# A long convolution and an attention on one core: four streams in the planner, sums by accumulating transfers, skip term in the first tap

## The chip, the core and the metric

The kernel runs on one core of a Trainium2 chip. A core has TensorE (PE; its weight loads are shown as PEld), VectorE (DVE), ScalarE (ACT), GpSimd (POOL) and SyncE (SP), each with its own instruction order, and 16 DMA engines that serve the queues of SP, ACT and POOL. Engines wait for each other through semaphores only. The metric is the device time of one execution in microseconds.

## What is computed

Two independent heads, joined in the last axis. The first is a long convolution: a kernel K of 2048 taps for each of 576 channels is made from a sum of 128 complex exponentials, and the input u is convolved with it, causally, with a skip term.

```
P = exp(logdA[:, :, None] * l)                       # D=576, N=128, L=2048
K = einsum("dn,dnl,dn->dl", Cc, P, dB).real
y = irfft(rfft(pad(u)) * rfft(pad(K)))[:L] + u * Dskip
```

The second is an attention over S=2048 with 32 query heads of 18 and one key and value head, fp32.

```
scores = einsum("bhqd,bkd->bhqk", q, k) * Dh**-0.5
o = einsum("bhqk,bkd->bhqd", softmax(scores), v);  out = o @ wo
```

## The kernel before

The attention runs over 4 chunks of 512 queries, 8 groups of 4 heads, 16 key blocks of 128 keys and 2 head pairs: 1024 score tiles (`pairs`). A score tile is two fp16 matmuls of 512 columns (L532) into one of 3 PSUM buffers; ScalarE makes exponentials of 1024 columns from it (L543); two half products of 256 columns (L845) add values times exponentials into `ops`. Beside this run the query projections (`qproj`), whose results go through DRAM by POOL's queue and come back as `aug` by SP's, and the output projections (`outproj`).

The convolution goes over 12 blocks of 48 channels (`Conv`). `front` (L1238) makes a block's kernel: `factors` (exponentials and sines on ScalarE once for two blocks, the second block parked in DRAM), `tables` (products on VectorE) and `kgen` (L1220; matmuls at L1231 into PSUM, copied to `ksb` by VectorE), then a trip through DRAM into `kt`. `back` (L1294) takes the forward transforms of the input and of the kernel (`transform`, L1263: TensorE matmuls lh, VectorE combinations `sc`), multiplies them in four taps (products `acc` and `pt`, sums of `pt` into `acc`, all on VectorE), combines three products into a complex one (`acc`, then `sv` and `w`), and takes the inverse transform (`iy`) to which the skip product `u` is added. Three accumulating transfers a block (L1303, L1316, L1338) and one plain (L1302) go by POOL's queue. All of it and the projections share one PSUM bank (`bank`, L235).

The order of the instructions on PE, ACT, DVE and POOL is fixed when the program is built, by a planner in the kernel itself. `Clock` keeps the planned time of TensorE (`t`), VectorE (`v`) and ScalarE (`a`). The works are generators (`Stream`): each yields before a step whether it is a TensorE step ("p"), a VectorE step ("v") or a wait ("w", "b"), and the time from which it is ready. `main` (L778) takes three score tiles a round, and between rounds `fill` (L801) puts in steps of the side work and the convolution as a credit allows. `turn` (L1396) runs the convolution as two streams, `back(k)` and `front(k+1)`, and starts the next pair when both have ended. Where VectorE copies out of the bank, the planned VectorE time is set to TensorE's (`evacuate`, L1255) and the copy is entered at once.

```
def evacuate(self):
    K = self.k
    K.v = max(K.v, K.t)
```

After the last product, what is left of the convolution is put in (`drain`, L1431), then `finish` (L642) normalizes the last heads and adds the last sums of the output.

Of the kernel before, what the change touches and what calls it, by code (L numbers as in the profile page):

```python
# [25 lines left out]
KT = [(k * 128, 128) for k in range(5)]  # L26
DT = KT[:4] + [(512, 64)]
# [11 lines left out]
LIMIT = 60.0  # L39

# [5 lines left out]
RATE = 6.983  # L46
PACE = 1.7672
AHEAD = 0.4952
TOTAL = 604.4861
LAST = 813.2825  # L50
DEFER = 0.378
NAUG = 5
LEFT = 1.1655
CAP = 1.5491
DEBT = 0.6604
GROUP = 0.1377
HOLD = 0.3071
LEAD = 1.8204
MOST = 0.4269
LEAST = 0.3048  # L60
NEAR = 1.3779
SLOPE = 0.851
SOON = 1.3672
URGENT = 8.8421
BACK = 2
HELD = 0
GAP = 0.2663
GAP_NEW = 0.3191
# [13 lines left out]

class Clock:
# [6 lines left out]
    def __init__(self):  # L90
        self.t = self.v = self.a = 0.0
        self.work = 0.0
        self.s = [0.0] * NS
        self.fill = 0.0
        self.due = self.last = 1e9

    def near(self):

        return NEAR if self.t + SOON > min(self.due, self.last) else 0.0

    def pe(self, cost, *after):
        self.t = max(self.t, *after) + cost if after else self.t + cost

    def act(self, cost, after=0.0):
        self.a = max(self.a, after) + cost
        return self.a

    def filled(self):

        self.fill = self.v + 0.25  # L110
        self.due = 1e9

    def dve(self, n, rate, after):
        cost = 0.068 + rate * n + (0.119 if after else 0.0)
        self.v += cost
        self.work += cost


class Vector:
# [5 lines left out]
    def cost(self, rate, out, *ins, n=None):  # L125

        place = lambda x: (x.name, x.offset)
        self.k.dve(math.prod((n or out).shape[1:]), rate, self.last in [place(x) for x in ins if hasattr(x, "offset")])
        self.last = place(out)
# [9 lines left out]
    def tensor_scalar(self, out, src, *a, **k):  # L139
        self.cost(0.527e-3, out, src, *a)  # L140
# [18 lines left out]
class Stream:  # L159
# [26 lines left out]
    def go(self, step, credit, lock=None):  # L186

        k = self.k
        ready = self.ready if self.kind != "p" or self.holds else max(self.ready, k.fill)
        if not self.live or self.kind == "b" or self.kind == "p" and (credit <= 0 or k.t < ready or lock not in (None, self)):  # L190
# [19 lines left out]
class Attention:  # L210
# [7 lines left out]
    def __init__(self, tc, ctx, aps, clock):  # L218
        self.tc, self.nc, self.a, self.k = tc, tc.nc, aps, clock
# [15 lines left out]
    def bank(self, n, name):  # L235
        self.k.pe(0.0, self.k.fill)
# [10 lines left out]
    def setup(self, tp, conv):  # L247
# [4 lines left out]
        self.sel = conv.con[:, 2 * NF:]  # L252
# [122 lines left out]
    def second(self):  # L375
# [3 lines left out]
        K.pe(0.86)  # L379
        self.last()  # L380
        K.pe(0.86)
        K.v = max(K.v, K.t)
# [6 lines left out]
    def maxima(self):  # L389
# [4 lines left out]
        K.pe(1.1)  # L394
        K.v = max(K.v, K.t)
# [4 lines left out]
    def values(self):  # L400
# [4 lines left out]
        K.pe(1.0)  # L405
        K.v = max(K.v, K.t)
# [8 lines left out]
    def qproj(self, c, m, xt):  # L415
# [5 lines left out]
        for f in range(n // 256):  # L421
            sl = slice(f * 256, f * 256 + 256)
            yield "p", K.fill, False
            ps = self.bank(256, f"q{c}_{m}_{f}")
            for k in range(5):
# [6 lines left out]
                K.pe(0.465)  # L432
                self.q_left -= 1
                self.units += 1
                K.due = K.t + 0.465 * (4 - k)
                if k < 4:
                    yield "p", 0.0, True
            K.v = max(K.v, K.t)
# [21 lines left out]
    def queries(self, c, m, qh, ql, aw):  # L460
# [18 lines left out]
        yield "p", max(K.v + 0.4, K.fill), False  # L479
# [10 lines left out]
        K.pe(0.15)  # L490
        K.v = max(K.v, K.t + 0.3)
# [33 lines left out]
    def scores(self, i, c, pr, kb, cost):  # L525
# [7 lines left out]
        K.pe(cost, K.s[i % NS])  # L533
        return ps, K.t + 0.27

    def exponentials(self, i, c, pr, kb, ps, ready, free):
        nc, K = self.nc, self.k
        K.s[i % NS] = K.act(0.925, max(ready, free)) + 0.1
# [7 lines left out]
    def gather(self, c, g, o_ps):  # L546
        nc = self.nc
        o_sb = self.p2.tile([P, CT], F32, tag="o", name=f"o{c}_{g}", bufs=1)
        self.k.v = max(self.k.v, self.k.t)
        self.V.tensor_copy(o_sb, o_ps)  # L550
        self.o_free = self.k.v + 0.3
        nc.sync.dma_start(self.od[c][g * P:(g + 1) * P, :], o_sb)

    def normalize(self, c, ms):
# [11 lines left out]
        yield "v", K.t + 6.0, False  # L566
# [6 lines left out]
        yield "v", K.v + 3.0, False  # L573
# [8 lines left out]
        for m in ms:  # L582
            mn = MT[m][1]
            yield "v", K.t + 5.0, False
            V.tensor_tensor(o[:mn, m, :], o[:mn, m, :], tiles[m][:mn, :], op=ALU.mult)
            self.scaled[m] = K.v + 0.3
# [3 lines left out]
    def outproj(self, c):  # L590
        nc, V, K = self.nc, self.V, self.k
        o = self.oT
        self.o_left += 40
        yield "p", max(self.scaled[4], K.fill), False
# [183 lines left out]
    def main(self, conv, flag):  # L778
# [81 lines left out]
        for r in range(0, len(pairs), NS):  # L860
# [45 lines left out]
            if r:  # L906
                fill(free())
# [643 lines left out]
```

## Time and profile before

| | us |
|---|---|
| median of three runs | 1216.06 (1213.11 to 1217.59) |
| the profiled execution | 1217.0 |
| its span, first to last instruction | 1215.2 |
| PE busy in the span | 1099.6 |
| ACT busy | 1035.3 |
| DVE busy | 961.1 |
| POOL busy | 95.5 |

The profile is of one execution. Busy time of an engine is the time in which one of its instructions ran; issuing transfers doesn't count as busy except on POOL. PEclk is the share of its full speed (2.4 GHz) that TensorE's clock was granted. In a row, `out<-in` names tiles by the names of the program, `Lnn` is a line of the kernel; the line can be that of a helper (L133 is every addition or product of two tiles on VectorE, L207 every matmul in four column strips).

### The profile page before, as it was taken

What the parts mean: (1) busy time and instruction counts of PE and PEld (TensorE: products, weight loads), DVE (VectorE), ACT (ScalarE), POOL (GpSimd) and SP (SyncE); (2) the same over time, 40 slices, a digit from 0 to 9 for tenths busy, and PEclk for the clock granted to TensorE, in tenths of its full rate; (3) what the DMA queues carried; (4) which work ended last, traced back from release to release, by engine and by line L of the source; (5) the groups of instructions that cost most, each with busy time, mean ns of one, the idle gap of its engine ahead of it and who ended that gap; (6) DMA issues with size and microseconds to landing.
All of it is one profiled execution on the core that took longest, in us unless ns stands there. A gap on an engine that the chain in (4) does not pass through costs nothing. (4 is left out here: it accounts for less than half of the span.)

```text
span 1215.2 us, 41325 instructions
## 1 busy us (share of the span) xinstructions
PE 1099.6 (90%) x17974; PEld 534.7 (44%) x17974; DVE 961.1 (79%) x1722; ACT 1035.3 (85%) x1092; POOL 95.5 (8%) x151
## 2 busy tenths in 40 slices
PE   7999999899999899999989999986789998999924
PEld 2454454345445344545444545432344543454412
DVE  7868979977975885995989596873779589869875
ACT  5899899899889978999999999999689999999700
POOL 1010201110110100110010000020000000000000
PEclk9999999999999999999999999998899999999967
DMA  8432343343323324322341312232042124241122
GB/s 295 130 121 69 105 118 90 113 134 110 91 58 97 97 74 154 103 66 89 95 165 49 120 51 82 75 80 110 21 149 58 69 67 151 72 130 42 46 66 68
DMA packets 54253, 117.87 MB, mean 97 GB/s; under 512 B 7628, under 2 KB 24925, under 8 KB 52787
## 3 DMA queue, kind: packets, MB, share of 16 engines
q1 hardware_dynamic: 43571, 88.62, 21.6%
q0 software_dynamic: 10064, 26.19, 9.3%
q8 instruction: 143, 2.34, 0.8%
q10 hardware_dynamic: 432, 0.37, 0.1%
q14 instruction: 43, 0.35, 0.1%
HBM read 54.58 MB, written 41.46 MB: 79 GB/s over the span
## 5 line engine op out<-in xcount | busy, mean ns | idle before, releaser
L543 ACT ACTIVATE P<-s 128x1024 f32<-128x1024 f32 x992 | 938.9, 1036 | 95.5 <-PE s L532 90.0
L845 PE MATMUL ops<-P,v_sb 128*32 128x256 f32 x8192 | 536.6, 383 | 4.1 <-DVE o L137 3.6
L845 PEld LDWEIGHTS ops<-P,v_sb 128*32 128x32 f32 x8192 | 247.2, 110 | 187.3 <-issue 53.2
L532 PE MATMUL s<-aug,kaug 55*128 55x512 f16 x2048 | 303.2, 382 | 28.8 <-ACT P L543 25.6
L532 PEld LDWEIGHTS <-kaug 55*128 55x128 f16 x2048 | 95.2, 94 | 248.4 <-issue 202.1
L207 PE MATMUL op<-wo_sb,oT 126*32 126x288 f32 (+1 forms) x1128 | 84.7, 417 | 8.3 <-DVE ob L137 5.9
L207 PE MATMUL q<-x,wq_sb 128*32 128x256 f32 x1200 | 80.1, 395 | 7.4 <-DVE un L145 4.2
L137 DVE COPY ksb<-kg 128x192 f32<-128x192 f32 x48 | 17.4, 363 | 70.9 <-PE kg L1231 70.9
L207 PE MATMUL iy<-w,dft_sb 128*32 128x192 f32 x768 | 40.8, 344 | 24.6 <-DVE w L133 23.8
L133 DVE TENSOR_TENSOR tab<-tab,tt 128x576 f32<-128x576 f32 (+1 forms) x72 | 59.1, 821 | 1.5
L133 DVE TENSOR_TENSOR tab<-sum,r 128x576 f32<-128x576 f32 (+1 forms) x72 | 58.8, 817 | 0.0
L133 DVE TENSOR_TENSOR tt<-f,sum 128x576 f32<-128x576 f32 (+1 forms) x72 | 58.8, 817 | 0.0
L133 DVE TENSOR_TENSOR tab<-r,dif 128x576 f32<-128x576 f32 (+1 forms) x72 | 58.8, 816 | 0.0
L133 DVE TENSOR_TENSOR tab<-tab 128x576 f32<-128x576 f32 (+1 forms) x72 | 58.7, 815 | 0.0
L133 DVE TENSOR_TENSOR acc<-acc,pt 128x864 f32<-128x864 f32 (+2 forms) x72 | 54.4, 755 | 1.7
L133 DVE TENSOR_TENSOR pt<-us,ks 128x864 f32<-128x864 f32 (+2 forms) x72 | 54.2, 753 | 0.8
L207 PEld LDWEIGHTS q<-x,wq_sb 128*32 128x32 f32 x1200 | 36.8, 113 | 40.6 <-issue 13.2
L207 PEld LDWEIGHTS op<-wo_sb,oT 126*32 126x32 f32 (+1 forms) x1128 | 32.4, 111 | 47.3 <-issue 10.7
L1231 PE MATMUL kg<-tab 128*32 128x64 f32 x2304 | 42.9, 224 | 9.0 <-DVE tab L133 7.2
L1302 POOL DMA_DIRECT2D us<-us x12 | 6.7, 559 | 510.4 <-issue 227.0
L1231 PEld LDWEIGHTS kg<-tab 128*32 128x32 f32 x2304 | 37.8, 113 | 20.4 <-DVE tab L133 7.8
L676 ACT ACTIVATE o_last<-ops 128x256 f32<-128x256 f32 x2 | 0.8, 384 | 53.5 <-issue 51.9
(169 smaller groups left out, 1055.0 us busy)
## 6 DMA issues: line engine op xcount, KB each, us to landing
park<-two SPq DMA_DIRECT2D x6, 1944.0 KB
us<-us POOLq DMA_DIRECT2D x24, 384.0 KB, 3.9
od<-o SPq DMA_DIRECT2D x31, 256.0 KB
aug<-qd SPq DMA_DIRECT2D x124, 54.0 KB
u<-u SPq DMA_DIRECT2D x12, 480.0 KB
kd<-ksb SPq DMA_DIRECT2D x12, 384.0 KB
kt<-kd SPq DMA_DIRECT2D x48, 96.0 KB
ks<-ks POOLq DMA_DIRECT2D x12, 384.0 KB, 4.8
```

The source lines that it names most:

```text
L133: return self.v.tensor_tensor(out, a, b, **k)
L137: return self.v.tensor_copy(out, src)
L207: nc.tensor.matmul(ps[j:e], w[:, j:e], x, start=start, stop=stop, tile_position=(0, j))
L532: nc.tensor.matmul(ps[:, j, :], self.kaug[r, kb * P:(kb + 1) * P], t[r, :], start=True, stop=True)
L543: nc.scalar.activation(pt, ps, AF.Exp, scale=SCALE / UNIT ** 2)
L676: nc.scalar.activation(o_sb[:, half[f]], o_ps[:, half[f]], AF.Copy)
L845: nc.tensor.matmul(o_ps[32 * j:32 * j + 32, cs], self.v[:, kb, :], pts[2 * n + j // 2][:, j % 2, cs], start=(kb + f == 0), stop=(kb + f == ...
L1231: nc.tensor.matmul(ps[32 * g:32 * g + 32, d, :], t[:, :32], t[:, 32:], start=(j == 0), stop=(j == 1), tile_position=(0, 32 * g))
L1302: nc.gpsimd.dma_start(us[:, 0:4, :], us[:, 4:8, :])
```

## The change

The planner's `Clock` gets a time for every engine and for transfers: it keeps for each part of each tile when it was written and read last, with a cost for a transfer by bytes and rows. A stream's readiness is asked of it (`K.at`). A copy out of the bank is a step of its own ("v", held): the bank stays with the stream until the planned matmuls have ended, and steps of other streams for VectorE may come before it. The loop goes by score tiles; `fill` enters, in this order, VectorE steps of all streams, TensorE steps of the convolution, of a side work begun, and products. The convolution runs as four streams: `fronts`, `inputs` (forward transform of u), `kernels` (forward transform of K) and `backs`, each through all blocks; `kt` has two buffers. `transform` leaves two of four combinations to accumulating transfers, and the back part its sums over the taps and four more combinations; the tap products become six instructions. The skip term is added to the first tap of the kernel (`tap`), and the input's copy of it is no longer loaded. The columns of a block are in another order so that the parts are contiguous. The inverse transform's TensorE steps are half as long.

```
--- before.py
+++ after.py
...
 class Clock:
...
+    def dma(self, q, out, src, add):
+        t = self.begin(0, self.g if q == "g" else self.t, out, (src,) + ((out,) if add else ()))
+        if q == "g":
+            self.g = t = t + 0.56
+        elif q == "s":
+            self.q = max(self.q, self.t, self.lanes[0]) + 0.45
+            t = max(t + 0.45, self.q)
+        size = mybir.dt.size(out.dtype)
+        n = math.prod(out.shape)
+        t += (3.3 if q == "g" else LAND) + max(n * size / 1.9e5, n / min(run(out), run(src)) * 4.4e-3)
+        self.end(0, t, out, (src,), HOP)
...
 class Stream:
...
     def go(self, step, credit, lock=None):
...
-        if self.kind == "v" and (k.t < self.ready or k.v > k.t + self.ahead - k.near()):
+        if self.kind == "v" and (max(k.t, k.v) < self.ready - EPS or k.v > k.t + self.ahead):
             return False
...
     def qproj(self, c, m, xt):
...
-            K.v = max(K.v, K.t)
+            yield "v", K.at(ps), True
             V.tensor_scalar(qh[:, sl], ps, UNIT, None, op0=ALU.mult)
...
     def main(self, conv, flag):
...
+        def pump():
+
+            while any(st.go(self.step, -1.0, holder()) for st in [x for x in (holder(),) if x] + [prep, side, conv]):
+                pass
...
+        def fill(i):
+
+            free = max(K.s[(i + j) % NS] - 0.225 * j for j in range(NS)) - 0.113
+            late = free + SLACK
+            while True:
+                pump()
+                left = late - K.t
+                if conv.go(self.step, left + LET, holder()):
+                    continue
+                if i - behind < FEW and beside(left, False):
+                    continue
+                if i - behind < NEW and behind_plan() and beside(left, True):
+                    continue
+                if behind < len(pairs) and ripe() <= K.t + 0.02 and left > ROOM:
+                    product()
+                    continue
+                if beside(left, False) or beside(left, True):
+                    continue
+                if K.t >= free:
+                    return
...
-        for r in range(0, len(pairs), NS):
-            new = range(r, min(r + NS, len(pairs)))
-            self.step = new[-1] // 2
...
+        for i, (c, g, kb, j) in enumerate(pairs):
+            self.step = i // 2
...
+            if i >= 2 and i % NS == 0:
+                fill(i)
...
 class Conv:
...
     def kgen(self, k, s, ksb):
...
-            K.pe(0.665)
-            self.evacuate()
-            self.V.tensor_copy(ksb[:, :, s, :, ds], ps.rearrange("p d (h c) -> p h c d", h=4))
+            K.pe(0.665, ps, (self.tab,))
+            yield "v", K.at(ps), True
+            self.V.tensor_copy(ksb[:, :, s, :, d0:d0 + TB // 2], ps.rearrange("p d (h c) -> p h c d", h=4))
             self.evacuated()
+        tap = ksb[:, 0, s, 0, :]
+        self.V.tensor_tensor(tap, tap, self.skip[:, k, s, :], op=ALU.add)
...
     def front(self, k):
...
-        while self.kt is not None:
+        while len(self.kt) == 2:
             yield "w", 0.0, False
-        kt = self.p1.tile([P, 4, NSB, 16, TB], F32, tag="kt", name=f"kt{k}")
+        kt = self.p1.tile([P, 4, NSB, 16, TB], F32, tag="kt", name=f"kt{k}", bufs=2)
...
     def transform(self, src, pick, y, nm):
...
-                self.evacuate()
+                yield "v", K.at(ps), True
...
-        V.tensor_tensor(y[:, 0:8:4, :], a, c, op=ALU.add)
-        V.tensor_tensor(y[:, 2:8:4, :], a, c, op=ALU.subtract)
-        yield "v", 0.0, False
-        V.tensor_tensor(y[:, 1:8:6, :], bd[:, 0:2, :], bd[:, 2:4, :], op=ALU.add)
-        V.tensor_tensor(y[:, 3:6:2, :], bd[:, 0:2, :], bd[:, 2:4, :], op=ALU.subtract)
+        V.tensor_tensor(y[:, 2:7:4, :], y[:, 0:5:4, :], y[:, 8:10, :], op=ALU.subtract)
+        nc.gpsimd.dma_start(y[:, 0:5:4, :], y[:, 8:10, :], accum_op=ALU.add)
+        yield "v", 0.0, False
+        V.tensor_tensor(y[:, 3:6:2, :], y[:, 1:8:6, :], y[:, 10:12, :], op=ALU.subtract)
+        nc.gpsimd.dma_start(y[:, 1:8:6, :], y[:, 10:12, :], accum_op=ALU.add)
...
-    def back(self, k, kt):
+    def spectrum(self, k, kt):
...
+        yield from self.transform(kt, lambda r: kt[:, :, :, 4 * r:4 * r + 4, :].rearrange("p g s b d -> p b (g s) d"), ks, f"k{k}")
+        self.kt.pop(0)
...
         nc.gpsimd.dma_start(ka, k2, accum_op=ALU.add)
...
+    def back(self, k):
...
-                    t = p1.tile(shp, F32, tag="sc", name=f"pt{k}_{m}_{h}")
-                    tt(t, at(us, 0, 4 - m), kb, op=ALU.mult)
-                    yield "v", 0.0, False
-                    tt(at(acc, m, 4), at(acc, m, 4), t, op=ALU.add)
...
-        tt(ut, ut, dsk.unsqueeze(1).broadcast_to([P, 4, NE]), op=ALU.mult)
...
+        for m, t in enumerate((acc, t1, t2, t3)):
+            for h in (slice(0, 4), slice(8, 12), slice(4, 8)) if m == 0 else (slice(0, 12),):
+                yield "v", max(K.at(us[:, h], ks[:, h]), K.free(blk(t[:, h], 0, 4 - m))), False
+                tt(blk(t[:, h], 0, 4 - m), blk(us[:, h], 0, 4 - m), blk(ks[:, h], m, m + 1).broadcast_to([P, h.stop - h.start, 4 - m, n]), op=ALU.mult)
+            if m == 1:
+                nc.gpsimd.dma_start(acc[:, :, n:], t1, accum_op=ALU.add)
+        self.us_free = self.ks_free = True
+        nc.gpsimd.dma_start(t2[:, :, n:], t3, accum_op=ALU.add)
+        nc.gpsimd.dma_start(acc[:, :, 2 * n:], t2, accum_op=ALU.add)
+        nc.gpsimd.dma_start(acc[:, 0:4, :], acc[:, 8:12, :], accum_op=ALU.add)
+        yield "v", K.at(acc[:, 4:12, :]), False
+        tt(acc[:, 4:8, :], acc[:, 8:12, :], acc[:, 4:8, :], op=ALU.subtract)
...
+        tt(bd[:, 0:4:3, :], acc[:, 4:6, :], acc[:, 6:8, :], op=ALU.subtract)
+        nc.gpsimd.dma_start(acc[:, 4:6, :], acc[:, 6:8, :], accum_op=ALU.add)
+        yield "v", K.at(acc[:, 0:4, :]), False
+        tt(bd[:, 1:3, :], acc[:, 0:2, :], acc[:, 2:4, :], op=ALU.subtract)
+        nc.gpsimd.dma_start(acc[:, 0:2, :], acc[:, 2:4, :], accum_op=ALU.add)
+        yield "v", 0.0, False
+        tt(w[:, 1:4:2, :], bd[:, 0:2, :], bd[:, 2:4, :], op=ALU.subtract)
+        nc.gpsimd.dma_start(bd[:, 0:2, :], bd[:, 2:4, :], accum_op=ALU.add)
+        yield "v", K.at(acc[:, 0:6, :]), False
+        tt(w[:, 0:3:2, :], acc[:, 0:5:4, :], acc[:, 1:6:4, :], op=ALU.subtract)
+        nc.gpsimd.dma_start(acc[:, 0:5:4, :], acc[:, 1:6:4, :], accum_op=ALU.add)
...
-                K.pe(0.65)
-                K.due = K.t
-                if r % 2 == 0:
-                    yield "p", 0.0, True
-            self.evacuate()
-            tt(ut[:, sl, :], ut[:, sl, :], ps, op=ALU.add)
+                    K.pe(0.33, ps, (acc[:, 0:5:4], d))
+                    if (r % 2, j) != (1, 1):
+                        yield "p", 0.0, True
+            yield "v", K.at(ps), True
+            V.tensor_copy(out[:, 2 * hf:2 * hf + 2, :], ps)
...
-        self.streams = [Stream(self.front(0), self.k)]
+        self.us, self.ks, self.us_free, self.ks_free = {}, {}, True, True
+        self.streams = [Stream(g, self.k) for g in (self.fronts(), self.inputs(), self.kernels(), self.backs())]
...
-            self.streams = [Stream(self.back(k, self.kt), self.k)] if k < NCK else []
-            if k + 1 < NCK:
-                self.streams.append(Stream(self.front(k + 1), self.k))
...
```

## Rows read from the trace of the kernel before

**Rows 1.** The page's busy times of each engine, in us, with the share of the span.

```profile
PE 1099.6 (90%) x17974; PEld 534.7 (44%) x17974; DVE 961.1 (79%) x1722; ACT 1035.3 (85%) x1092; POOL 95.5 (8%) x151
```

**Rows 2.** Busy us by stage: stretch, length, PE, PEld, DVE, ACT, POOL, PEclk, DMA share, GB/s.

```profile
25.80:1149.60 1123.80, 1054.02 (x17332) 514.73 (x17336) 901.12 (x1611) 1020.61 (x1074) 87.44 (x135) 0.98 0.31 94
500.00:600.00 100.00, 97.78 (x1664) 49.10 (x1661) 84.95 (x160) 93.99 (x101) 12.97 (x21) 1.00 0.30 84
700.00:800.00 100.00, 97.49 (x1620) 47.16 (x1613) 82.42 (x144) 92.11 (x99) 8.45 (x12) 1.00 0.26 73
830.00:870.00 40.00, 23.80 (x329) 10.43 (x319) 26.52 (x43) 28.24 (x29) 0.00 (x0) 0.79 0.17 67
1149.60:1198.80 49.20, 16.08 (x336) 9.24 (x332) 32.25 (x54) 0.00 (x0) 3.13 (x4) 0.69 0.23 57
1198.80:1215.20 16.40, 9.92 (x160) 5.53 (x152) 8.00 (x16) 0.77 (x2) 0.00 (x0) 0.95 0.27 100
```

**Rows 3.** Waits of ACT, 28 to 1148 us: us in total, times, longest.

```profile
ACT P L543 <- PE s L532: 90.0, 155, 10.1
```

**Rows 4.** Source view of L1231: ns minimum, median, maximum, first and last start.

```profile
L1231 PE MATMUL kg<-tab x2304: 218/219/316, 62.4 to 1153.6; 128*32 128x64 f32 x192
```

**Rows 5.** Waits of DVE for PE, 28 to 1148 us: first two, last of nine.

```profile
DVE ksb L137 <- PE kg L1231: 68.9, 35, 3.0
DVE u L133 <- PE iy L207: 32.4, 16, 5.3
...
DVE sck L137 <- PE hk L207: 3.2, 3, 2.2
```

**Rows 6.** Groups by form on DVE: count, busy us, mean ns, idle before.

```profile
L133 DVE TENSOR_TENSOR acc<-us,ks 128x1152 f32<-128x1152 f32 x24 | 32.4, 1352 | 0.9 <-DMA ks<-ks 0.7
...
L133 DVE TENSOR_TENSOR acc<-acc,pt 128x864 f32<-128x864 f32 x24 | 25.3, 1053 | 0.4
...
L133 DVE TENSOR_TENSOR sv<-acc 128x384 f32<-128x384 f32 x48 | 24.4, 547 | 2.9 <-DMA acc<-acc 2.9
...
L133 DVE TENSOR_TENSOR acc<-acc,pt 128x576 f32<-128x576 f32 x24 | 18.1, 755 | 0.6
...
L133 DVE TENSOR_TENSOR u<-u 128x768 f32<-128x768 f32 x12 | 11.4, 950 | 0.0
...
L133 DVE TENSOR_TENSOR acc<-acc,pt 128x288 f32<-128x288 f32 x24 | 11.0, 457 | 0.7
...
L133 DVE TENSOR_TENSOR w<-raw 128x48 f32<-128x48 f32 x24 | 4.8, 201 | 0.0
```

**Rows 7.** Source view of L1338, accumulating transfers of 384 KB: issue ns, landing us.

```profile
L1338 POOL DMA_DIRECT2D acc<-acc x12: 844/885/946, 144.0 to 1187.7; - x12
...
DMA to landing us min/median/max: 3.9/4.3/9.4
```

**Rows 8.** The page's DMA queue of POOL: packets, MB, share of 16 engines.

```profile
q0 software_dynamic: 10064, 26.19, 9.3%
```

**Rows 9.** Timeline from 1123 us on: start, us, engine, line, operation, idle before.

```profile
1123.29 0.88 PE L1231 MATMUL kg<-tab 128*32 128x64 f32 x48
...
1149.40 1.48 PE L207 MATMUL iy<-w,dft_sb 128*32 128x192 f32 x32
...
1154.27 0.86 PE L207 MATMUL hu<-u,dft_sb 128*32 128x192 f32 x16 [0.48 <-DVE ksb L137]
...
1175.48 1.36 DVE L133 TENSOR_TENSOR acc<-us,ks 128x1152 f32<-128x1152 f32 x1
...
1193.25 2.79 PE L207 MATMUL iy<-w,dft_sb 128*32 128x192 f32 x32 [23.50 <-DVE w L133]
...
1198.76 0.14 DVE L926 TENSOR_SCALAR flag<-u 1x1 int32<-1x1 f32 x1
```

**Rows 10.** Waits of PE, 28 to 1148 us: us in total, times, longest.

```profile
PE s L532 <- ACT P L543: 25.6, 47, 5.8
PE kg L1231 <- DVE tab L133: 7.2, 1, 7.2
```

More of the change, by code (lines that the diff above doesn't have):

```diff
@@ L80, with run @@
 HALF_PI = 1.5707963
+HOP = 0.075
+FIRST = 27.8301
+FETCH = 4.3
+ROOM = 0.3724
+INTO = 0.113
+BACK = 0.104
+EPS = 0.0209
+def run(x):
+    n = 1
+    for step, m in reversed(x.ap[1:]):
+        if step != n:
+            break
+        n *= m
+    return n
 class Clock:
     def __init__(self):
-        self.t = self.v = self.a = 0.0
-        self.work = 0.0
+        self.t = self.v = self.a = self.g = self.q = 0.0
+        self.work = self.fill = 0.0
+        self.n, self.block, self.since, self.mode = 0, 0, -1e9, 0
@@ L93, in __init__ @@
         self.s = [0.0] * NS
[L94 to L105, printed above, removed]
-        return self.a
-    def filled(self):
[L110 to L116, printed above, removed]
+        self.table = None
@@ new lines, in at, with free, begin @@
+    def at(self, *xs):
+        return max([float(c[0][c[3]].max()) for c in map(self.cells, xs) if c] or [0.0])
+    def free(self, *xs):
+        return max([float(np.maximum(c[0][c[3]], c[1][c[3]]).max()) for c in map(self.cells, xs) if c] or [0.0])
+    def begin(self, e, t, out, ins):
+        for x in ins + ((out,) if out is not None else ()):
+            c = self.cells(x)
+            if c:
+                t = max(t, float(np.where((c[2][c[3]] == e) & (e > 0), 0.0, c[0][c[3]]).max()))
+                if x is out:
+                    t = max(t, float(c[1][c[3]].max()))
+        return t
@@ new lines, in end, with turn, pe @@
+    def end(self, e, t, out, ins, lag):
+        for x in ins:
+            c = self.cells(x)
+            if c:
+                c[1][c[3]] = np.maximum(c[1][c[3]], t + HOP)
+        c = self.cells(out) if out is not None else None
+        if c:
+            c[0][c[3]], c[2][c[3]] = t + lag, e
+    def turn(self, mode):
+        if mode != self.mode:
+            self.t += INTO if mode else BACK
+            self.mode = mode
+    def pe(self, cost, out=None, ins=()):
+        self.fetch()
+        self.turn(0)
+        self.t = self.begin(1, self.t, out, tuple(ins)) + cost
+        self.end(1, self.t, out, tuple(ins), 0.166 + HOP)
@@ L906, in main @@
-            if r:
-                fill(free())
-            c, g, kb, j = pairs[new[-1]]
-            self.group = (new[-1] + 1) // 32
+            while (i - NP) // 2 >= behind // 2:
+                product()
+            pts[i] = self.exponentials(i, c, 2 * g + j, kb, *ps, read.get((i - NP) // 2, 0.0))
+            done[i] = K.a
+            if j == 0:
+                continue
+            self.group = (i + 1) // 32
             self.fetch(self.group)
```

517 lines of the change are left out of this document (268 added, 249 removed).

## Prediction

> **What bounds the kernel now.** I read the busy times of the engines first [rows 1]: TensorE is busy 1099.6 of 1215.2 us, ScalarE 1035.3, VectorE 961.1. Three engines are that full, so the share alone settles nothing, and I cut the span into stages [rows 2]. From 25.8 us (first scores) to 1149.6 us (last product of attention) TensorE is busy 1054.0 of 1123.8 us (93.8%), ScalarE 1020.6, VectorE 901.1. This stage is TensorE's: the waits of ScalarE [rows 3] show 90.0 us for scores, so ScalarE, which is at 91%, is mostly the one that waits. Then comes a stage of 49.2 us, 1149.6 to 1198.8, in which ScalarE does nothing and TensorE 16.1 us at a granted clock of 0.69 of the full 2.4 GHz: the last convolution block alone. 16.4 us of finish follow; 1.8 us lie outside the span (execution 1217.0 us, median of the runs 1216.06, so the profiled one stands for them).
>
> Why is the convolution late? The matmuls that make its kernels (L1231) begin at 62.4 us for the first of 12 blocks [rows 4] and at 1123.29 for the last [rows 9]: one block in (1123.3 - 62.4)/11 = 96.4 us. VectorE is 80% busy but not free in the rest: of its 222.7 us idle in the stage (1123.8 - 901.1) about 190 are waits for TensorE in the order of its queue: nine kinds, from 68.9 us for the kernel's sums and 32.4 for the inverse transform down to 3.2 [rows 5]. The planner of before puts the copy out of PSUM into VectorE's order at once and VectorE stands until TensorE has got there. Busy and blocked together VectorE is 97% taken: it sets the convolution's pace, and TensorE the stage's.
>
> **Part 1: sums moved from VectorE to transfers.** By the forms [rows 6], for one block. Taken out: the sums of the taps, 2 x (1.053 + 0.755 + 0.457) = 4.53 us; two of four combinations in each of the two forward transforms, and in the back part two of the four sv and two of the four w, all of 384 elements like the sv row, 8 x 0.547 = 4.38; the skip product of 768 elements 0.95. The products of the taps go from eight instructions (2 x (1.352 + 1.053 + 0.755 + 0.457) = 7.23, the smaller three taken at the sums' times of the same sizes) to six: three of 768 elements (3 x 0.95, the skip product's row of that size), one of 1152 (1.35), one of 576 (0.755), and one of 1728, of which there is no row; 1152 to 864 elements is 0.30 us, so I extend by that to 1.95. That is 6.9, 0.3 less. Added: two additions of 6 elements to the first tap. No row is that small; between nothing and the 0.20 of 48 elements [rows 6], I take 0.20 each. Net -9.8 us a block, -117 us in all: VectorE 961 to about 844. As VectorE isn't the stage's bound, this is worth time only through the convolution's pace.
>
> What it adds: GpSimd issues 15 transfers a block (4 in the transforms, 2 for the input, 1 for the kernel, 8 in the back part) for 4 now. At 0.88 us each [rows 7] that is 11 x 12 x 0.88 = 116 us on an engine with 95.5 busy [rows 1]: covered, if the engine's order holds nobody up (rival C). Bytes: 4800 KiB a block for 1536, so 40 MB more. 26.19 MB of that queue took 9.3% of the DMA engines' time [rows 8]; 40 MB would take 14% more, and the engines are at 31% [rows 2]: covered. Latency: an accumulate of 384 KB lands after 3.9 to 9.4 us, median 4.3 [rows 7]. Those with 12 short rows in each partition (864, 288 and 576 KB) have no row. Their ends are 4.3 us (size costs nothing) and 4.3 x 864/384 = 9.7; I take 9, 6 and 7, near the upper end because their rows are short. Chain of one block in the back part: products 6.9, then 9 (288 KB beside it), 7, 4.3, a difference 1.0, then three accumulates of about 4 with differences of 0.5 to 1.1 between: about 42 us to the inverse transform, for 17.8 now (1175.48 to 1193.25 [rows 9]). This is hidden as long as other streams have work. The loads that move (the parked half and the input, on SP, now a stage of work earlier) wait for what they waited for before and cost nothing while no engine waits for them; at the head the constants' tile grows by 72 KB, under 0.8 us at the stage's 94 GB/s [rows 2], beside loads that end later.
>
> The Trainium skill's page "DMA: Bandwidth & Descriptors", section "Anatomy of one DMA", fits such a transfer as 2.0 us plus its bytes at 436 GB/s; the largest would then land in about 4 us (an estimate by that page) and the chain would be some 12 us shorter. The row of 384 KB (4.3 us measured, 2.9 by the fit) is above it.
>
> **Part 2: copies out of PSUM entered when TensorE is done, four streams.** The copy now waits as a step of its stream until the planner's TensorE has finished; other streams' VectorE work goes ahead. The PSUM bank stays taken meanwhile, and only the holder may use it; products fill TensorE. If none of the blocking goes, the pace is 96.4 - 9.8 = 86.6 us a block; from the last block's first kernel matmul to its end it is 75.5 us now (1123.3 to 1198.8), 24 more with the longer chain, and the convolution ends near 62.4 + 11 x 86.6 + 99.5 = 1114 us, about when attention's products do. If half of the 190 us goes (8 a block), 78.6 us and about 1027. Either way the stage of 49.2 us loses its reason, though the first case has no margin (rival B). The inputs and kernels of the next block run beside the back part of this one, which before they didn't: the last block then enters the end with its transforms done.
>
> The 49.2 us go, and the last block's TensorE work moves into the busy stage: 2 x 0.88 (kernel) + 8 x 0.86 (forward) + 3 x 1.48 (inverse, with the half of block 10 at 1149.40) = 13 us at the full clock's rows [rows 9]; some of it overlaps at its ends, so 12. Gain of this part 49 - 12 = 37.
>
> **Part 3: order of TensorE's work.** The stage holds one large stall. From 830 to 870 us TensorE is busy 23.8 of 40 and its granted clock falls to 0.79, after it had stood 5.8 us behind ScalarE's sines and 7.2 us behind tables that VectorE hadn't finished [rows 2, 10]. At 95% and this clock it would be 15 us shorter (40 - 23.8/0.95); at the full clock, by an estimate from the 0.79, some 5 more. The new planner gives the cover of sines and tables its own times, so such a place can go or turn up elsewhere: I count 12 of the 20. Outside it TensorE is at (1054.0 - 23.8)/(1123.8 - 40) = 95.1%, and 97.8 and 97.5% in the two best stretches [rows 2]. If all ran like these, the stage would gain 2.6% of 1084, 28 us; if nothing changes, none. With VectorE less full and its copies sooner I take half, 14. Shorter units of the inverse transform (0.33 us) and of the score loop cost nothing by themselves: the same matmuls in another order. ScalarE's 1020.6 us stay below the result.
>
> Sum: 1217.0 - 37 - 12 - 14 = 1154. As a check: first scores 25.8 + stage 1123.8 + 12 - 12 - 14 = 1110 + finish 16.4 + 1.8 = 1154. TensorE would be at 96%.
>
> **Rivals.** A, the better end: TensorE runs as in its best stretches and the stall is gone whole: 1217 - 37 - 20 - 28 = 1132; with the granted clock at 1.00 for the stage's 0.98 (up to 22 us at full load), down to 1112. For it: two stretches of 100 us that already do so with a block of convolution each. Against: everything must go well.
>
> B, the convolution is still late, the change does not do what it says. One PSUM bank serves all four streams and is now held until the copy is in order; if that costs what the blocking cost, the pace stays near 90 to 92 us, the convolution ends about 1150 to 1175 and the longer chain (42 us for 17.8) stands uncovered at the end. The 49 us shrink to about 30: 1217 - 19 - 6 = 1192. With only the tail gone and no denser stage: 1180. For it: the bank is still one, and streams are asked in the order of VectorE work done, so that `fronts`, which has most, comes last. Against: the 117 us taken from VectorE don't depend on the order.
>
> C, slower: landings later than the planner reckons. It puts TensorE's inverse transform where the model says that the accumulates have landed, and TensorE takes its work in order, so a late landing stops scores and products behind it. In the drain one such wait is 23.5 us [rows 9]; in the stage there are none now. The chain has five accumulates one after another, and GpSimd's queue puts query stores behind them. If each lands 1.5 to 2 us late (the row's maximum is 5.1 over its median [rows 7]), 8 us a block are paid: 12 x 8 = 96 against the 63 gained: 1250. It decides from 63/12 = 5.2 us a block, about 1 us an accumulate.
> The Trainium skill's page "SBUF — State Buffer", section "SBUF: two separate sides", gives a way for this: while VectorE runs a copy between two fp32 tiles of SBUF, GpSimd can't write its descriptors, and a transfer of 620 ns took 3100. The trace doesn't bear it out so far: the issue of acc takes 844 to 946 ns in all 12 blocks [rows 7], with VectorE at 80%.
>
> **How the numbers follow.** Forecast case (1135 to 1175) 0.48; A (1112 to 1135) 0.14; B and the tail alone (1175 to 1211) 0.16; near no change, 1211 to 1223, 0.06; C (over 1223) 0.16. Half a percent, 6 us, is about what a measurement of this kernel tells from no change: faster 0.78, same 0.06, slower 0.16. The time is the likeliest case's, 1154. The range 1112 to 1220 leaves out C and little else.
>
> **What would show it.** Right: ScalarE's exponentials end within 25 us of the span's end; kernel matmuls (L1231's successor) begin a block every 78 to 87 us and stop before 1060; VectorE busy 835 to 855; its waits for the kernel's sums and transforms below 100 us; TensorE's busy share of the stage 95 to 97%. Wrong: TensorE waiting at the inverse transform or for scores on a transfer (C), a stage at the end without ScalarE over 20 us (B), or GpSimd's issues well above 0.9 us for the transfers with short rows.

## The result and the profile after

The kernel after takes 1224.26 us in the median of 20 runs (1213.02 to 1229.18), the kernel before 1215.93 in as many (1213.11 to 1219.74). The ratio is 1.0049, with an interval of 1.0033 to 1.0065: a little slower, where 1154 was forecast. The profiled execution took 1218.73 us, 5.5 below that median, so the views of after show rather too little of the loss.

Busy times and the DMA queues of after (packets, MB, share of the 16 engines' time), to be read beside [rows 1, 8]:

```profile
span 1217.0 us, 41419 instructions
PE 1126.8 (93%) x17974; PEld 543.6 (45%) x17974; DVE 860.7 (71%) x1545; ACT 1037.3 (85%) x1092; POOL 265.6 (22%) x283
...
q0 software_dynamic: 87440, 66.31, 36.6%
q1 hardware_dynamic: 43571, 87.44, 21.3%
```

q0 is GpSimd's queue, q1 SP's. VectorE lost 100 us of work (117 forecast) and GpSimd's queue got 40 MB more, as reckoned. Not as reckoned is the queue's share of the DMA engines: 36.6% for the 9.3 + 14 forecast. The stages of after, in the view by windows (length; busy time and instructions of PE, PEld, DVE, ACT, POOL; granted clock, DMA share, GB/s), cut about 1 us behind the last product of attention, for [rows 2]:

```profile
25.80:1202.20 1176.40, 1097.94 (x17692) 534.31 (x17692) 833.47 (x1487) 1022.98 (x1075) 260.51 (x270) 0.97 0.59 125
1202.20:1217.00 14.80, 8.43 (x128) 3.88 (x118) 7.16 (x13) 0.39 (x1) 0.00 (x0) 0.92 0.25 85
```

The stage of 49.2 us in which the last block ran alone is gone. But attention's stage, 1123.8 us long before, is now 1176.4. TensorE's idle time in it rose from 69.8 to 78.5 us, its busy time from 1054.0 to 1097.9. ScalarE's waits for scores rose from the 90.0 us of [rows 3]:

```profile
L693 ACT ACTIVATE P<-s 128x1024 f32<-128x1024 f32 x992 | 940.8, 1029 | 147.9 <-PE s L245 144.5
```

What VectorE waited for on transfers (us in total, times, longest; over the whole view these are 54.6 us, 10.1 in the kernel before):

```profile
DVE oT L280 <- DMA db<-rden: 17.1, 7, 5.8
DVE ob L284 <- DMA outb<-ob: 10.3, 2, 6.0
DVE r__11498 L280 <- DMA sum__11499<-park: 7.1, 1, 7.1
DVE r__14163 L280 <- DMA sum__14164<-park: 6.5, 1, 6.5
```

None of these four is a transfer of the change: they are SP's (denominators, the output, the parked half block). Where TensorE falls back most, one sees the chain, here from 1084 to 1110 us on VectorE, TensorE and ScalarE:

```profile
DVE oT L280 <- DMA db<-rden: 10.3, 2, 5.8
...
PE op L245 <- DVE us L280: 6.8, 1, 6.8
...
ACT P L693 <- PE s L245: 9.2, 4, 7.8
```

VectorE stands behind the denominators; work of the convolution that is queued behind on VectorE is late, so TensorE, in its order, stands 6.8 us at the output projection, which needs the bank, and ScalarE gets no scores for 7.8 us.

The issue of the two largest new transfers on GpSimd (groups of instructions; busy us, mean ns), and the landing of new transfers (DMA issues; KB each, median us):

```profile
L230 POOL DMA_DIRECT2D acc<-t x24 | 43.9, 1827 | 234.1 <-issue 82.0
```

```profile
acc<-t POOLq DMA_DIRECT2D x12, 864.0 KB, 10.9
...
acc<-t POOLq DMA_DIRECT2D x12, 576.0 KB, 7.7
acc<-acc POOLq DMA_DIRECT2D x36, 192.0 KB, 5.2
...
t<-t POOLq DMA_DIRECT2D x12, 288.0 KB, 11.1
```

Those with 12 short rows in a partition take 1.83 us to issue, for 0.88 of [rows 7].

### The profile page after: what moved, and what is told of

It reads as the page before. It is cut to its first block, busy times and chain, and to the rows that moved or that the text cites. A ratio compares the mean times of both kernels' runs of the same rounds, so it can differ in the third digit from the quotient of the medians.

```text
span 1217.0 us, 41419 instructions
## 1 busy us (share of the span) xinstructions
PE 1126.8 (93%) x17974; PEld 543.6 (45%) x17974; DVE 860.7 (71%) x1545; ACT 1037.3 (85%) x1092; POOL 265.6 (22%) x283
## 3 DMA queue, kind: packets, MB, share of 16 engines
q0 software_dynamic: 87440, 66.31, 36.6%
## 5 line engine op out<-in xcount | busy, mean ns | idle before, releaser
L693 ACT ACTIVATE P<-s 128x1024 f32<-128x1024 f32 x992 | 940.8, 1029 | 147.9 <-PE s L245 144.5
L245 PE MATMUL ops<-P,v_sb 128*32 128x256 f32 x8192 | 565.7, 388 | 14.1 <-DVE o L284 8.1
L245 PEld LDWEIGHTS ops<-P,v_sb 128*32 128x32 f32 x8192 | 254.0, 110 | 237.5 <-issue 78.4
L230 POOL DMA_DIRECT2D acc<-t x24 | 43.9, 1827 | 234.1 <-issue 82.0
L230 POOL DMA_DIRECT2D acc<-acc x48 | 51.5, 1116 | 170.1 <-DVE w L280 80.9
L230 POOL DMA_DIRECT2D ks<-ks x36 | 39.5, 1251 | 210.6 <-DVE ks L280 194.9
L230 POOL DMA_DIRECT2D us<-us x48 | 49.7, 1215 | 128.1 <-DMA us<-us 77.1
L245 PEld LDWEIGHTS q<-x,wq_sb 128*32 128x32 f32 x1360 | 40.7, 109 | 35.2 <-issue 10.1
L230 POOL DMA_DIRECT2D qd<-qh x46 | 28.5, 686 | 100.6 <-DVE qh L288 100.5
L280 DVE TENSOR_TENSOR t<-us,ks 128x1728 f32<-128x1728 f32 (+2 forms) x36 | 47.6, 1350 | 0.0
L284 DVE COPY o<-ops 128x512 f32<-128x512 f32 x31 | 21.3, 687 | 34.6 <-PE ops L245 34.3
L280 DVE TENSOR_TENSOR ks<-ks 128x384 f32<-128x384 f32 (+2 forms) x60 | 41.8, 713 | 0.8
## 6 DMA issues: line engine op xcount, KB each, us to landing
acc<-t POOLq DMA_DIRECT2D x12, 864.0 KB, 10.9
```

What stands on the lines that cost most here:

```text
L230: return self.q.dma_start(out, src, **k)
L245: return self.e.matmul(out, w, x, **k)
L280: return self.v.tensor_tensor(out, a, b, **k)
L284: return self.v.tensor_copy(out, src)
L693: nc.scalar.activation(pt, ps, AF.Exp, scale=SCALE / UNIT ** 2)
```

## First set: the sums back on VectorE

Four theories stood after the result. Chain: landings between a block's tap products and its inverse transform hold the convolution back. Contention: the transfers make other transfers late. Late exponentials: products are entered at the moment at which the planner has their exponentials ready. And order alone: any change of the plan shuffles 41000 instructions.

**e1.** All eleven new accumulates a block become additions.

```
-        nc.gpsimd.dma_start(t2[:, :, n:], t3, accum_op=ALU.add)
+        tt(t2[:, :, n:], t2[:, :, n:], t3, op=ALU.add)
```

> The kernel after with its eleven new accumulating transfers a block (four in the forward transforms, three over the taps, four in the back part) written as additions on VectorE again; streams, planner and skip term as after. Chain theory: after the change the back part is one loop through one acc buffer, and from a block's first tap product to its inverse transform it takes 44 to 83 us, mostly landings, so a block can't come faster than about 88 us; with sums of 0.5 to 1.1 us in place of landings of 5 to 11 us this falls to 25 to 45 us, the pace to 78 to 84 us a block although VectorE is at about 960 us, and the time to 1190 to 1207. Contention theory (transfers make other transfers late, VectorE stands): VectorE's waits for DMA fall from about 50 to about 10 us, TensorE's stalls behind them go, 1207 to 1215. Late exponentials theory (products entered with no reserve, TensorE waits inside them about 45 us): nothing changes, 1218 to 1230. The prediction's own view that VectorE's relief is what pays: 1235 or more.

1191.16 us, ratio 0.9793 [0.9773, 0.9813]: with all of VectorE's work back the kernel is 31 us faster than after (1.0049 - 0.9793 = 2.6%), and 25 faster than before. The prediction's own view, that VectorE's relief is what pays, had 1235 or more. Busy times of e1, and its stage up to the last product:

```profile
PE 1110.5 (93%) x17974; PEld 536.8 (45%) x17974; DVE 955.9 (80%) x1677; ACT 1037.0 (87%) x1092; POOL 93.7 (8%) x151
```

```profile
25.80:1176.40 1150.60, 1082.28 (x17698) 527.79 (x17698) 929.16 (x1620) 1022.73 (x1075) 88.62 (x138) 0.99 0.31 94
```

The chain theory has the time, but not its reason: the inverse transforms' first kind of matmul (`iy` from `acc`) starts first at 169.6 us and last at 1143.6, 88.5 us a block; in after at 226.5 and 1192.9, 87.9 a block. The chain got shorter and the pace did not.

**e2 and e3** split the eleven: only the three sums over the taps on VectorE, or only the other eight.

> Only the three sums over the taps (864, 288 and 576 KB in rows of 576, 192 and 384 bytes) back on VectorE; the other eight accumulates a block stay transfers. Chain theory: two of the chain's landings (11 and 8 us) become 1 to 2 us each, the loop of a block is some 16 us shorter: 1195 to 1212. Contention theory: these three are most of the packets (the queue's share should fall from 36.6 to about 18%), so nearly all of what the first kernel of this set wins, 1207 to 1215. Late exponentials: 1218 to 1230.

1203.61 us, 0.9891 [0.9867, 0.9915], share of the queue 19.7%.

> The complement: the eight sums with long rows (four in the transforms, four in the back part) back on VectorE, the three over the taps stay transfers. Chain theory: three landings of about 5 us and one of us or ks leave the loop: 8 to 14 us shorter, 1205 to 1218. Contention theory: the packets stay, 1217 to 1228. Late exponentials: 1218 to 1230.

1236.93 us, 1.0178 [1.0156, 1.0200], share 25.7%: slower than after, which no theory had.

**e4** sizes what order does by itself.

```
-CLEAR = 1.9054
+CLEAR = 1.8
```

> The kernel after with one constant of its planner changed (CLEAR 1.9054 to 1.8, how near a convolution step may be for a new side step to start): the same instructions in another order. It sizes what a reshuffled order alone does. If order alone is worth under 10 us: 1214 to 1234. If the order found for after is a lucky one among many: 1240 to 1290, with the same work on every engine and more idle time on TensorE and ScalarE.

1269.04 us, 1.0442 [1.0416, 1.0468]. Nearly the same instructions (VectorE's are 1529 for 1545) in another order cost 45 us more. So a comparison of kernels with different orders, e1 to e3 among them, can't bear a reading of ten or twenty microseconds by itself, and even e1's 31 us is less than this; e3 stays inconclusive. The third set therefore keeps the order.

## Second set: latency, traffic, reserve

**e5** is e1, with the planner told that each sum lands as late as the transfer would. **e6** is e1 with the same traffic beside it, into a tile in DRAM. **e7** is after with a reserve of 0.3 us for products.

```
 e5:
+        for o, i in ((acc[:, :, n:], t1), (t2[:, :, n:], t3), (acc[:, :, 2 * n:], t2)):
+            K.dma("g", o, i, True)
 e6:
+        nc.nc.gpsimd.dma_start(self.rows[48], t3, accum_op=ALU.add)
 e7:
-                if behind < len(pairs) and ripe() <= K.t + 0.02 and left > ROOM:
+                if behind < len(pairs) and ripe() + TRAIL <= K.t + 0.02 and left > ROOM:
```

> The instructions of e1 (all eleven sums on VectorE, no transfer added), but the planner is told that each of these sums lands as late as the transfer would; so only the order of the instructions differs from e1, and it has the latency of the kernel after without its traffic. Chain theory (the latency between a block's tap products and its inverse transform delays the convolution, so that TensorE lacks its work and has it later): first tap product to inverse transform 60 us and more again, the convolution ends with or behind attention, 1215 to 1245. Contention theory (the transfers themselves cost, by being many): order alone costs little, 1190 to 1202.

1221.6 us, 1.0050 [1.0032, 1.0067]: an order made for the latency costs 30 us against e1 without one transfer more. That is less than e4's order cost, so the number alone says little. Where the time goes, the windows of e5 show:

```profile
25.80:1173.00 1147.20, 1077.59 (x17412) 519.18 (x17412) 903.38 (x1579) 1021.87 (x1074) 87.98 (x136) 0.98 0.30 92
1173.00:1205.00 32.00, 11.70 (x204) 6.95 (x196) 21.30 (x29) 0.77 (x2) 1.69 (x2) 0.68 0.19 50
```

Attention ends at 1173, as in e1, and a block of convolution is left: TensorE 11.7 of 32 us, ScalarE nothing. That is not how after loses its time, whose convolution ends with attention.

> The order of e1 with all sums on VectorE, and beside them eleven accumulating transfers a block of the sizes and row lengths of the kernel after, issued at the same places by GpSimd from the same kinds of tiles into a tile in DRAM that nobody reads (no room is left for it in SBUF): traffic and issue without anybody waiting for the sums. Contention theory: other transfers land late, VectorE waits for them 40 us and more, 1205 to 1222. Chain theory: 1190 to 1200. Were it the issue on GpSimd that holds VectorE's writes up, VectorE's busy time would rise above the 956 us of e1.

1421.71 us, 1.1682 [1.1645, 1.1718]; VectorE's waits for transfers 243 us, its busy time 959.9, hardly above e1. It doesn't isolate the traffic, as was meant: the sources of the added transfers are written again soon, so VectorE waits for the transfers themselves, and real accumulates stand behind them on GpSimd.

```profile
DVE w L280 <- DMA acc<-acc: 100.4, 10, 17.3
DVE ks L284 <- DMA spare<-ks: 85.8, 12, 7.7
```

> The kernel after, where a product of values and exponentials is entered only when its exponentials have been ready for 0.3 us in the planner's time instead of at the moment they are. Late exponentials theory (TensorE stands some 45 us between a product's matmuls because the exponentials come a little later than planned, 12 us before): that wait falls below 15 us and the time to 1190 to 1208. If this wait is only the place where TensorE waits for ScalarE anyway: the wait moves to the scores or to idle time, and with less to choose from the order is worse, 1220 to 1255.

1233.75 us, 1.0140 [1.0110, 1.0170]. TensorE's weight loads of a product wait for exponentials, a wait that the kernel before doesn't have at all, and which the reserve makes shorter, from the first row (after) to the second (e7):

```profile
PEld ops L245 <- ACT P L693: 23.4, 50, 4.5
```

```profile
PEld ops L246 <- ACT P L694: 16.3, 46, 0.8
```

The longest falls from 4.5 to 0.8 us, and ScalarE waits 159.1 us for scores, for 144.5. Late exponentials are a place at which TensorE waits, and this reserve does not win the time back. As e7 is another order too, its 1233.75 doesn't price these waits; but they aren't what after lost: e8, next, has them in full (23.6 us, by the same view) and is 38 us faster.

## Third set: the same order, with fewer transfers

Leaving transfers out, while the planner still reckons with them, keeps the order of after on TensorE, VectorE and ScalarE. In the traces of after and e8 the instructions of VectorE and ScalarE follow each other alike, tile by tile. Then the difference is what the transfers cost on the chip. **e8** leaves out all eleven, so the output lacks their sums; **e9** too, but the planner is not told of them.

```
 e8:
-        nc.gpsimd.dma_start(t2[:, :, n:], t3, accum_op=ALU.add)
+        K.dma("g", t2[:, :, n:], t3, True)
 e9:
-        nc.gpsimd.dma_start(t2[:, :, n:], t3, accum_op=ALU.add)
+        pass
```

> The kernel after without its eleven new accumulating transfers a block (their sums are left out, the output lacks them); the planner still reckons with them, so the order of the instructions on TensorE, VectorE and ScalarE is that of the kernel after, instruction for instruction. What the transfers cost on the chip beyond the order that was made for them is the difference to 1224. Chain theory: most of the loss is in the order, so 1208 to 1224. Contention theory: late landings and issues of 1.8 us are what stretches the stage, 1180 to 1200.

1185.47 us, 0.9739 [0.9712, 0.9766]: in the range that contention named. With one order the transfers cost 1.0049 - 0.9739 = 3.1%, 38 us.

```profile
25.80:1170.00 1144.20, 1084.45 (x17686) 528.51 (x17686) 832.67 (x1488) 1022.64 (x1075) 89.67 (x138) 0.99 0.31 94
```

Against after the stage is 32.2 us shorter: TensorE idles 18.7 us less (59.8 for 78.5) and is busy 13.5 less, at a granted clock of 0.99 for 0.97. The four waits of after are there, at the same instructions, and about half as long (25.0 us over the whole view for 54.6):

```profile
DVE oT L280 <- DMA db<-rden: 7.5, 5, 2.8
DVE ob L284 <- DMA outb<-ob: 5.3, 2, 3.2
DVE r__11409 L280 <- DMA sum__11410<-park: 4.1, 1, 4.1
DVE r__14054 L280 <- DMA sum__14055<-park: 3.8, 1, 3.8
```

Laid on each other matmul by matmul, the two traces drift apart in jumps: 29 us come in five places of after, 164 to 176, 792 to 804, 840 to 852, 1032 to 1044 and 1088 to 1108 us; small gains and losses elsewhere add 3. In the last four VectorE stands behind a late transfer (`outb`, the parked half twice, `db`), at 840 TensorE also 3.7 us behind an accumulate of its own. In the first the DMA share is high too (1.05, for 0.48 in e8), but no engine waits for a transfer by the trace; what costs its 4 us isn't shown.

Why they are late, the windows around two of these places show, each time after first and then about the same work in e8 (the last two columns are DMA share and GB/s):

```profile
1079.00:1091.00 12.00, 11.87 (x192) 5.96 (x192) 9.81 (x15) 11.03 (x12) 2.66 (x2) 1.00 1.18 188
1054.00:1063.00 9.00, 9.00 (x148) 4.58 (x146) 8.97 (x15) 8.29 (x10) 0.00 (x0) 1.00 0.44 126
...
787.00:799.00 12.00, 8.20 (x118) 3.30 (x109) 5.79 (x9) 9.08 (x10) 3.53 (x2) 0.97 1.07 154
779.00:789.00 10.00, 9.36 (x146) 4.12 (x138) 6.88 (x10) 8.93 (x11) 0.00 (x0) 1.00 0.34 99
```

The mean DMA share of after's stage is 0.59, but here the time of the packets adds up to more than the whole time of 16 engines (1.18 and 1.07), for 0.44 and 0.34 in e8. GpSimd had issued accumulates of 864 and 288 KB at 1078.03 and 1079.89 us. At this place SP's trip of the denominators before `db` is what lands late: SP's longest wait for it is 5.5 us in after (first row, 1076 to 1104 us) and 2.0 in e8 (second row, 1049 to 1073).

```profile
SPq L230 <- DMA rden<-dn: 8.6, 2, 5.5
SPq L230 <- DMA rden<-dn: 3.8, 2, 2.0
```

Where the parked half is loaded, the share is high in e8 as well (0.76 and 0.77, for 0.88 and 0.86 in after, 819 to 827 and 999 to 1008 us for 836 to 845 and 1021 to 1031), and VectorE waits there in both.

> The same eleven sums left out and the planner not told of them: neither VectorE work nor latency nor traffic for them (the output lacks them). Against e1 it measures what 100 us less VectorE work is worth by itself, on which part 1 of the prediction rested. By the prediction: the convolution's pace falls by 8 to 10 us a block and the time with it, 1150 to 1175. If VectorE at 80% isn't what holds the convolution or TensorE back: within 10 us of e1, 1180 to 1200, with the convolution's last matmul long before attention's.

1187.52 us, 0.9761 [0.9734, 0.9787]. Against e1 (0.9793) 96 us less VectorE work are worth 0.3%, within the intervals. The two have different orders, so this number alone would prove little; but the traces show where the relief went. VectorE's waits for TensorE, all kinds added from 28 us to the end of attention, are 152.5 us in e1 and 250.5 in e9: VectorE waits for TensorE as much longer as it works less. And the convolution, free of sums and landings, is done at 1034 us, with attention's last product still at 1167 (matmuls of the tile `iy`, their first and last start; the stage in the view by windows):

```profile
L245 PE MATMUL iy<-w,dft_sb x576: 326/326/528, 166.5 to 1033.9; 128*32 128x192 f32 x192
...
L245 PE MATMUL iy<-acc,dft_sb x192: 322/326/351, 165.0 to 1030.2; 128*32 128x192 f32 x192
```

```profile
25.80:1167.60 1141.80, 1078.91 (x17690) 529.16 (x17692) 832.13 (x1487) 1023.36 (x1075) 89.55 (x138) 0.99 0.31 94
```

So the convolution's pace, now (1030.2 - 165.0)/11 = 78.7 us a block, no longer sets the end of anything.

**e10** is the version to which this points: e1, with the planner's constants set anew (among them SLACK 0.4074 to 0.3136, LET -0.1 to -0.2297, URGENT 8.84 to 11.2).

> e1 (all sums on VectorE) with eleven constants of the planner set anew, so that its own reckoning ends 15 us earlier than that of e1. If the chip follows the plan as in the runs so far (attention's end 22 to 36 us behind it): 1172 to 1188, faster than both kernels. If the gain is only on paper: 1188 to 1215, with more waiting of TensorE for exponentials or copies.

1182.98 us, 0.9723 [0.9695, 0.9751]: faster than both kernels, 34 us under before, with the whole computation.

**e11 to e13** ask what in the transfers costs it, with the order of after.

```
 e13:
-                nc.gpsimd.dma_start(acc[:, :, n:], t1, accum_op=ALU.add)
+                K.dma("g", acc[:, :, n:], t1, True)
+                nc.nc.gpsimd.dma_start(acc[:, 0:9, :].rearrange("p q x -> p (q x)"),
+                                       t1.rearrange("p q x -> p (q x)"), accum_op=ALU.add)
```

> The order of the kernel after, instruction for instruction, with only the three accumulating transfers over the taps left out (1728 KB a block in 12 short rows of each partition; the output lacks these sums); the eight small ones stay. Leaving out all eleven won 39 us with this order. If the loss is the number of packets (37000 of the queue's 77000 new ones have under 512 bytes, and the taps make most of the rest): these three carry most of it, 1188 to 1200. If it is the number of transfers, or GpSimd's issues and waits in its order: eight of eleven are still there, 1203 to 1216.

1202.11 us, 0.9862 [0.9832, 0.9892].

> The complement with the same order: the eight small accumulates (192 to 384 KB in rows of 768 or more bytes) left out, the three over the taps stay. Packets theory: 1208 to 1222. Number of transfers theory: 1192 to 1204.

1209.43 us, 0.9937 [0.9906, 0.9968].

> The order of the kernel after and all eleven transfers, but the three over the taps move the same bytes between places that are contiguous in each partition, one long row in place of 12 (so they add wrong elements). If the short rows are what fills the DMA engines: the queue's share falls from 36.6 to under 26%, the largest transfer lands after some 6 us for 10.9, and the time is 1192 to 1208. If bytes count: share and time stay within 3 points and 8 us, 1214 to 1226.

1216.46 us, 0.9993 [0.9969, 1.0016]. The landing of the largest transfer in e13, its queue, and that transfer's issue:

```profile
acc<-t POOLq DMA_DIRECT2D x12, 864.0 KB, 7.3
```

```profile
q0 software_dynamic: 36752, 66.31, 28.5%
```

```profile
L1459 POOL DMA_DIRECT2D acc<-t x12 | 10.3, 860 | 123.7 <-DVE t L280 64.7 <-issue 35.1 <-PE s L245 11.6
```

The five kernels of one order (the waits are the sum over the view of VectorE's waits for transfers; the ratio is to the kernel before):

| | packets | share of q0 | waits, us | ratio |
|---|---|---|---|---|
| all transfers (after) | 87440 | 36.6% | 54.6 | 1.0049 |
| long rows (e13) | 36752 | 28.5% | 49.1 | 0.9993 |
| the three over the taps (e12) | 65936 | 26.5% | 45.7 | 0.9937 |
| the eight small (e11) | 31568 | 19.7% | 38.6 | 0.9862 |
| none (e8) | 10064 | 9.3% | 25.0 | 0.9739 |

The parts add up: the taps 1.9%, the small ones 1.1%, all 3.1%. Neither packets (e13 has half of e12's and is slower) nor the number of transfers (three cost more than eight) orders the rows; the time that the queue takes of the DMA engines does, and VectorE's waits go with it: from 9.3 to 36.6%, 38 us, 1.4 us a point. GpSimd's issues don't order the rows either: POOL is busy 199.9 us in e11 and 159.7 in e12, which is the slower. Bytes (66.3 MB in the first two rows, then 47.4, 45.1 and 26.2) give the same order, but for the first two rows, which differ by 0.6%. Shares and waits are of one execution each, and the profiled one of e13 (1220.78) was slower than that of after (1218.73), though its median is lower.

Of the expectations, e11 fell between its two ranges and e12 into that of packets. e13's time is in the range for bytes (1214 to 1226), but its share fell by 8 points, neither under 26% nor by less than 3: short rows are a third of what the taps cost (0.6 of 1.9%), bytes and the transfer as such the rest.

## Why the prediction was wrong, step by step

- **VectorE's relief**: 844 us forecast, 860.7 measured. The size was right within 16 us; that it is worth time was not. e9 against e1: 0.3%, with the relief come back as waits for TensorE.
- **Transfers "covered" by engines at 31%**: this is the step that failed, with a price of zero for 38 us. The share of the queue was scaled by bytes (14% for 40 MB) and is 27. And a mean share isn't cover: around an accumulate the engines were full (1.18 and 1.07 for the mean of 0.59). What they delay are SP's transfers, for which VectorE stands in its order. Rival C had the mechanism (a late landing, an engine in order, TensorE stopped) with 1250, in the wrong place: TensorE's waits at the inverse transform are few, 3.7 us the longest on an accumulate. My point of decision, 1 us of lateness an accumulate, looked at the new transfers alone.
- **Landings** of 9, 6 and 7 us for 864, 288 and 576 KB: 10.9, 11.1 and 7.7. **Issue** of 11 x 12 x 0.88 = 116 us: POOL is busy 265.6 for the 211 that this gives, as short rows take twice as long.
- **Part 2**: right in size. In e9, which pays nothing for sums, the time from attention's last product to the end of the span falls from 65.6 to 15.3 us, 50 for the 49 forecast; in after itself to 15.7. The reason given for it didn't hold: VectorE's waits for TensorE, which were to shrink from about 190 us or at worst stay, are 260 in after (all kinds added, 28 to 1200 us). That the tail went all the same is in part luck; what of the four streams did it wasn't tried.
- **Part 3**, -26 for the stall and a denser order: wrong. In e9 the stage is 1141.8 us, 18.0 longer than before, and 12 of these are the moved work: +6. TensorE's idle time is 62.9 for 69.8; its busy time grew 13 more than the moved work; whether the new waits for exponentials lie in this isn't shown. I had taken two good stretches of the old order as what the new one would hold throughout.
- **Hidden chain**: it was hidden, but at the price of VectorE's relief: with the sums on VectorE the same latencies cost 30 us (e5 against e1), without them none (e8 against e9), as far as kernels of different orders can tell.
- **Rival B**: the pace was 87.9 us a block by the inverse transforms and (1064.6 - 74.5)/11 = 90.0 by the kernel matmuls (86.6 forecast if none of the blocking went, 90 to 92 in this rival), but the pace isn't the bound.

As a sum: 1154, and 32 for part 3 (26 not won and 6 lost) make 1186, with 1187.5 measured in e9 and 1185.5 in e8; the transfers' 38 make 1224, measured 1224.26. The 32 are read off e9's own trace and the 38 are after less e8, so that the sum closes proves nothing more; of the two the 38 were isolated by experiment, the 32 were not.

**Signs named in the prediction**: exponentials end 17 us before the span's end (right, below 25); VectorE outside 835 to 855; kernel matmuls a block every 90 us and until 1104.9 (78 to 87, and before 1060); VectorE's waits for the kernel's sums and transforms 121 us (below 100); TensorE busy 93% of the stage (95 to 97); issues of the short rows well above 0.9 us, one of the three signs of being wrong. TensorE's own waits on transfers, for which the prediction told to look, were small and would not have given the cause; VectorE's did.

**What stays open**: why the plan of after, even without transfers, leaves ScalarE waiting 113 us for scores, 23 more than before. e7 and e10 show that it depends on the planner's constants; which rule of it does this wasn't found. Of e3's 1237 us the order's and the transfers' parts weren't separated. That SP's transfers were taken off the path by themselves, with the traffic left in, wasn't tried.

## What to carry over

A transfer that takes work off a busy engine isn't free because the DMA engines' mean share is low: look at the share in the stretch around each transfer, and at which other engine waits, in its order, for any transfer of any queue, and price the delay there. To tell an order from the cost of what is ordered, take the operation out and leave the order as it is; where a planner fixes the order, comparing two plans alone can mislead by more than the effect. And before work is moved off an engine, take that work out altogether once: if the time stays, and the engine only waits longer for another, there is little to gain.

## What the runs showed of the hardware

Between SBUF tiles, an accumulating transfer with 12 rows of 576 bytes in a partition took 1.83 us to issue and 10.9 to land; the same 864 KB as one long row took 0.86 and 7.3, and the queue's share of the engines fell from 36.6 to 28.5%, with three of eleven transfers changed. The Trainium skill's page "DMA: Bandwidth & Descriptors", section "Why small descriptors are slow (HBM only)", has it that transfers between SBUF tiles don't suffer from small descriptors; for these the runs show otherwise.

GpSimd's 46 query stores, untouched by the change, took 686 ns to issue in after, and 554 in e8 and in e1 alike: so it was the other transfers, not VectorE (71% busy in after, 80 in e1), that made them slower. For these stores this speaks against the mechanism of VectorE's copies holding GpSimd's descriptors up, which the prediction had weighed from the page "SBUF — State Buffer" of the Trainium skill, section "SBUF: two separate sides".
